# The order of the first attention pairs, and where V's parts and the weights' work are issued, in an attention-then-MLP kernel

## The chip, the core and the metric

The kernel runs on one core of a Trainium2 chip. The metric is the device time of one execution in microseconds (us); lower is better. The engines are named TensorE (PE), VectorE (DVE), ScalarE (ACT), GpSimd (POOL) and SyncE (SP); SP issues the DMAs.

## The reference

Windowed attention with a distance bias over 8 batches, 8 heads, 576 positions and head size 64, followed by an MLP on the 4608 tokens:

```python
scores = scale * q @ k.T                       # per batch and head
rel = pos[:, None] - pos[None, :]
scores = where((rel >= 0) & (rel < 128), scores - slope[h] * abs(rel), -1e9)
attn = softmax(scores)
x = (attn @ v).transpose(0, 2, 1, 3).reshape(4608, 512)
h = x @ w_in                                   # 512 -> 2048
g = h * sigmoid(h)
out = g @ w_out                                # 2048 -> 512
```

All inputs and the output are float32.

## The kernel before

The tokens are cut in 36 blocks of 128 (two batches make nine blocks). A *pair* p is four of the eight heads of block p // 2; there are 72 pairs. Four blocks (512 tokens) are a *group* g of the MLP; there are nine groups. The MLP of a group goes over 16 feature blocks f of 128: gemm1 makes h of the block in PSUM, act1 to act4 make g from it as a high part gh and a low part gl, and gemm2 adds the block's share to four PSUM banks w, x, y, z. Precision comes from splitting numbers in two parts and summing three products of parts.

Nothing is ordered by a scheduler. All is written out by hand as *steps*: `plan` maps a step's number to a list of functions, `put(step, fn, ...)` appends to it, `later(n, ...)` appends n steps ahead, and `begin()` issues the list of the present step. Each engine works its own instructions off in the order in which they were issued. Steps below 0 hold the attention of the first eight pairs alone (at(0) is step -82, each pair 8 steps on, at(7) is -26). From step 0 on, each step also holds half a gemm1 or half a gemm2, 64 steps to a group, while the attention of the next group's pairs runs between them. Within a step the functions of the pair loop come first, in order of the pairs, then those put further down.

A first pair (p < 8) goes through `scores` at n = at(p), `row_max` (adds the bias from `tab` and takes the maximum, VectorE), `exps` (ScalarE), `p_transpose_first` (TensorE, in float32, into PSUM bank h), `p_copy_first` (unit u = 0 on ScalarE, u = 1 on VectorE, into hl), `attend` (the products of the transposed weights with V and a column of ones, in float32) and `normalize`. The tiles t that row_max fills have three buffers, and a pair takes two. `x_transpose` then turns x for the first group, cc 0 and 1 from the even pairs' heads and 2 and 3 from the odd ones'; `x_low` makes its low part. Pairs from 8 on use halves in 16 bits instead: `p_hi`, `p_lo`, `p_transpose` (a DMA), and V in two parts, `v_hi` (GpSimd) and `v_lo` (VectorE). `load_v` brings V for them. Pair 8 starts at `CLOSE[0]`.

V's parts need a scale of V over a batch pair b: `vscale_load`, `vscale_reduce` (a chunk's maximum), and `vscale_finish` in three stages: reduce (VectorE, `vcol`), transpose (TensorE, `vt`, line 237) with a few small VectorE steps on one number, and a spreading matmul (TensorE, `vs`). `qk_load` and `qk_sum` gather statistics of q and k for later batches.

The 32 weight blocks are loaded and split while the first group's MLP runs, one by one, in the order of `wq`: `w_split1` and `w_low3` (ScalarE), `w_join` (VectorE), `w_hi` (ScalarE), `w_lo` (GpSimd). `w_next` starts one of them; `AHEAD` loads are issued before the MLP. At a group's last feature block, `turn_over` issues act2 to act4 and, where the next group needs it, `x_parts` at once.

The lines that set the order around the change:

```python
if p < 2 * GT:
    a = n + 2 * STEP + 1                         # attend of a first pair
put(n + STEP + 3, p_transpose_first, p, u)
put(n + STEP + 4, p_copy_first, p, u)
put(a - 3, v_hi, i); put(a - 2, v_lo, i)         # pairs from 8 on
seq += [("g1", n, 0)] + [("xt", 0, 2), ("xt", 0, 3)] * (n == 0) + [("g1", n, 1)]
if g == 0 and half == (n == 0):
    w_next()
```

Of the kernel before, what the change touches and what calls it, by code (L numbers as in the profile page):

```python
# [6 lines left out]
F32 = mybir.dt.float32  # L7
# [10 lines left out]
P = 128  # L18
# [36 lines left out]

IN16, OUT16 = 2, 3
QK16 = 2
STATS16 = ("w1_10", "w1_11")
RAW16 = ("w1_0", "w1_1")
Q16 = ("w1_2", "w1_3")  # L60
K16 = ("w1_4", "w1_5", "w1_6")
# [7 lines left out]
WHOLE = ("w1_12", "w0_13", "w0_14", "w1_13")  # L69
AHEAD = 12  # L70
KEPT = 6
WD = (1, 2, 3)

CLOSE = (1, 5, 8, 14, 20, 26, 32, 38)


def at(p):
# [9 lines left out]
def tile_window_attention_then_silu_mlp(ctx, tc, qk, qk16, v, w_in, w_out, base8, out):  # L87
# [86 lines left out]

    def vscale_load(b, i):

        t = early_tile(i) if b == 0 else pool.tile([P, DM], F32, tag="rv", bufs=2, name=f"vm{b}_{i}")
        nc.sync.dma_start(t, v[b, i * P : (i + 1) * P, :])
        vred.setdefault(b, {})[i] = t = t.rearrange("p (h d) -> p h d", h=H)
        if b == 0 and i < KEPT:  # L180
            rvs[i] = t

    def vscale_reduce(b, i):
# [6 lines left out]
        else:  # L190
            junk = pool.tile([P, H, D], F32, tag="gt", name=f"vj{b}_{i}")
            nc.scalar.activation(junk, t, AF.Abs, accum_out=m)

    def qk_load(b, i):

        if b == QK16:
            if i == 0:
                vred[b, "qk"] = pool.tile([P, 4, DM], F32, tag="xl", bufs=1, name=f"qs{b}")
            t = vred[b, "qk"][:, 2 * (i % 2) : 2 * (i % 2) + 2]
        else:  # L200
            t = pool.tile([P, 2, DM], F32, tag=STATS16[i % 2], bufs=1, name=f"qs{b}_{i}")
        nc.sync.dma_start(
            t.rearrange("p k (h c) -> p k h c", h=NHP), qk[b * NBLK + i].rearrange("k p h c -> p k h c")
        )
        vred[b, "qk", i] = t

    def qk_sum(b, i):

        t = vred.pop((b, "qk", i))
        for k in range(2):  # L210
            m = vred[b]["m"][:, (1 + k) * VCH + i : (1 + k) * VCH + i + 1]
            nc.scalar.activation(t[:, k], t[:, k], AF.Abs, accum_out=m)

    wsc = {}

# [9 lines left out]
    def vscale_finish(b, stage):  # L225

        if b >= QK16:
            scales16(b, stage)
            return
        r, name = vred[b], b  # L230
        if stage == 0:
            r["col"] = col = pool.tile([P, 3], F32, tag="vcol", name=f"vcol{name}")
            nc.vector.tensor_reduce(col[:, 0:1], r["m"], axis=AX.X, op=ALU.max)
        elif stage == 1:
            col = r["col"]
            ps = ps_of(next_tag("misc"), f"vt{name}")
            nc.tensor.transpose(ps[:1, :P], col[:, 0:1], ident)
            c = col[:1, 1:2]
            nc.vector.tensor_reduce(c, ps[:1, :P], axis=AX.X, op=ALU.max)
# [4 lines left out]
            nc.vector.tensor_scalar(c.bitcast(I32), c.bitcast(I32), -1, 268 << 23, op0=ALU.mult, op1=ALU.add)
        else:
            ps = ps_of(next_tag("misc"), f"vs{name}")
            nc.tensor.matmul(ps[:, 0:2], ones[:1, :], r["col"][:1, 1:3], start=True, stop=True)
            vsc[b] = pool.tile([P, 2], F32, tag="vsc", name=f"vsc{name}")
            nc.vector.tensor_copy(vsc[b], ps[:, 0:2])
            del vred[b]  # L250
# [255 lines left out]
    def attend(p):  # L506
        i, q = divmod(p, 2)
        o0 = blocks(p).start
        st[p]["av"] = av = ps_of(next_tag("av"), f"av{p}")[:, : 4 * (D + 1)].rearrange("p (h d) -> p h d", h=4)
        for u in range(2):  # L510
            if p < 2 * GT:
                for h in range(2):
                    for o in range(o0, 2):
                        nc.tensor.matmul(
                            av[:, 2 * u + h], st[p]["hl"][u][:, h * (2 - o0) + o - o0], vf[i - 1 + o][:, 4 * q + 2 * u + h],
                            start=o == o0, stop=o == 1, skip_group_check=True,
                        )
                continue
            hl = st[p]["hl"][u][:, : 4 * (2 - o0)].rearrange("p (a h o) r -> p a h o r", a=2, h=2)
            for h in range(2):  # L520
                seq = [
                    (hl[:, part, h, o - o0], vp[:, (i - 1 + o) % VSLOTS, 4 * q + 2 * u + h])
                    for o in range(o0, 2)
                    for part, vp in ((0, v1), (0, v2), (1, v1))
                ]
                for n, (lhs, rhs) in enumerate(seq):
                    nc.tensor.matmul(  # L527
                        av[:, 2 * u + h, : rhs.shape[-1]], lhs, rhs, start=(n == 0), stop=(n == len(seq) - 1),
                        skip_group_check=True,
                    )  # L530
# [276 lines left out]
    for p in range(NPAIR):  # L807
        i, q = divmod(p, 2)
        n = at(p)
        if p < 2 * GT:  # L810
            a = n + 2 * STEP + 1
        elif p == 2 * GT:
            a = n + 10
        elif p == 2 * GT + 1:
            a = n + 12
        else:
            a = n + (15 if p < 4 * GT else 13 if i < QK16 * NBLK else 12)
# [15 lines left out]
        if p < 2 * GT:  # L833

            for u in range(2):
                put(n + STEP + 3, p_transpose_first, p, u)
                put(n + STEP + 4, p_copy_first, p, u)
        else:
            put(n + 3, p_hi, p, 0)
            put(n + 4, p_lo, p, 0)  # L840
            put(n + 4, p_hi, p, 1)
            put(n + 4, p_transpose, p, 0)
            put(n + 5, p_lo, p, 1)
            put(n + 5, p_transpose, p, 1)
        put(a, attend, p)
        z = a + 1
        put(z, normalize, p, 0)
        put(z + 1, normalize, p, 1)
        put(z + 2, x_hi, p)
        put(z + 2, x_lo, p)  # L850
        if q == 0:
            if 1 < i < QK16 * NBLK:
                put(at(2 * i - 3) + 1, load_q, i)
                put(at(2 * i - 3) + 1, load_k, i)
            if i >= KEPT:
                put(n + 4, load_v, i)
            if i == GT:
                put(a - 5, v_hi, i - 1)
                put(a - 4, v_lo, i - 1)
            if i >= GT:  # L860
                put(a - 3, v_hi, i)
                put(a - 2, v_lo, i)
    for k in range(2 * NF):
        put(STATS + k, w_stat, k % 2, k // 2)
    for x, wait in enumerate((0, 2, 5)):
# [3 lines left out]
            for k, fn in enumerate((conv1, conv2, conv3)):  # L869
                put(n + SLICE * f + (CLEAR if f > 4 else 0) + (k if which or f else 0), fn, which, f)  # L870
    for g in range(1, NG):
        put(at(2 * GT * g) + 10, x_unit, g)
        if g >= IN16:
            put(g * SLICE * NF - 2, mlp_scales, g)
    for b in range(1, NBB):

        n = at(2 * GT * (NBLK * b // GT)) + 2
        for i in range(VCH):
            put(n - 53 + 5 * i, vscale_load, b, i)
            put(n - 49 + 5 * i, vscale_reduce, b, i)  # L880
            if b >= QK16:
                put(n - 52 + 5 * i, qk_load, b, i)
                put(n - 46 + 5 * i, qk_sum, b, i)
        for x, wait in enumerate((0, 2, 5)):
            put(n + wait, vscale_finish, b, x)

# [8 lines left out]
    def w_next_load():  # L895
        if wi[0] < len(wq):
            w_load(*wq[wi[0]])
            wi[0] += 1

    def w_next():  # L900
        if wi[1] < len(wq):
            a = wq[wi[1]]
            wi[1] += 1
            w_split1(*a)
            w_low3(*a)
            for fn, n in zip((w_join, w_hi, w_lo), WD):
                later(n, fn, *a)
            later(1, w_next_load)

    def begin():  # L910
# [3 lines left out]
    with tc.manual_schedule():  # L914
# [16 lines left out]
        for i in (2, 3):  # L931
            put(at(2 * i - 3) + 1, load_whole, i)
        for i in range(GT, VCH):
            put(at(4) + 3 + 3 * (i - GT), vscale_load, 0, i)
        for i in range(VCH):
            put(at(3) + 6 + 4 * i, vscale_reduce, 0, i)
        for x in range(3):
            put(at(7) + (6, 8, 16)[x], vscale_finish, 0, x)
        for n in range(AHEAD):
            put(at(1) + 4 + 5 * n, w_next_load)  # L940
        put(at(0) + 1, keep_warm, 6)
        put(at(1) + 1, keep_warm, 16)
        for n in (at(5) + 5, at(6) + 5, at(7) + 5):
            put(n, w_next)
        for cc in range(2):
            put(at(7) + 13 + cc, x_transpose, cc)
        put(at(7) + 14, x_low, 0)
        put(at(7) + 20, x_low, 1)
        while pos[0] < 0:
            begin()  # L950
            pos[0] += 1
# [2 lines left out]
        for g in range(NG):  # L954
# [2 lines left out]
            seq = []  # L957
            for f in range(NF):
                n = g * NF + f
                seq += [("g1", n, 0)] + [("xt", 0, 2), ("xt", 0, 3)] * (n == 0) + [("g1", n, 1)]  # L960
                if 0 < f < NF - 1:
                    seq += [("g2", n - 1, 0), ("g2", n - 1, 1)]
            n = g * NF + NF - 1
            seq += [("g2", n - 1, 0), ("g2", n - 1, 1), ("g2", n, 0), ("g2", n, 1)]
            for k, n, half in seq:
                if k == "xt":
                    x_transpose(half)
                    x_low(half)
                    continue
                begin()  # L970
                x_send()
                if k == "g1":
# [61 lines left out]
```

## Time and profile before

| what | value |
|---|---|
| median of 3 runs | 951.65 us (951.18 to 952.29) |
| the profiled execution | 949.61 us, span 947.8 us |
| TensorE busy | 921.9 us, 97% |
| VectorE busy | 655.0 us, 69% |
| ScalarE busy | 558.9 us, 59% |
| GpSimd busy | 133.5 us, 14% |
| DMA | 123.28 MB, mean 130 GB/s |
| chain that ended last | TensorE 78%, ScalarE 5%, VectorE 5%, issue 2% |

The span runs from the first to the last instruction of the program; the execution's time is a little longer. A row of a timeline gives start and duration in us, engine, line and operation, output <- input, the number of instructions merged in it, and in brackets how long the engine had been idle and what released it. Matmuls overlap in these rows, so their cost is read from start to start.

### The profile page before, as it was taken

The numbers are of one execution on the slowest core, as the hardware profiler recorded it, in microseconds if no ns is written. First come the engines' busy times: TensorE is split into PE (matmuls) and PEld (weight loads), VectorE is DVE, ScalarE is ACT, GpSimd is POOL, SyncE is SP. The second block draws the span as 40 slices with busy tenths as digits, with TensorE's granted clock in tenths as the row PEclk, the third lists the DMA queues.
The fourth block names the chain that finished last, engine by engine and source line by source line (L and its number), as shares of the span: only waits on it lengthen the run. The fifth ranks groups of instructions, "written<-read, shape, count | busy, mean of one in ns | idle before, by whom it ended". The sixth has DMA issues, their size and how long they took to land.

```text
span 947.8 us, 17110 instructions
## 1 busy us (share of the span) xinstructions
PE 921.9 (97%) x6442; PEld 574.9 (61%) x6442; DVE 655.0 (69%) x1603; ACT 558.9 (59%) x1152; POOL 133.5 (14%) x122
## 2 busy tenths in 40 slices
PE   8799999999999999999999999999999999999998
PEld 7677777777778888555545555555555545554443
DVE  4687887555778887899687778776777777743222
ACT  5678888676555674666567756555655565532222
POOL 0145665121212221000000000000000000000000
PEclk9999999999999999999999999999999999999999
DMA  9949942423277762644597765544654554421001
GB/s 277 375 119 246 272 101 67 106 65 87 65 181 200 166 142 50 156 101 101 111 244 179 221 144 132 118 112 98 139 111 104 119 142 106 87 55 56 1 1 44
DMA packets 209266, 123.28 MB, mean 130 GB/s; under 512 B 172576, under 2 KB 180768, under 8 KB 209184
## 3 DMA queue, kind: packets, MB, share of 16 engines
q1 hardware_dynamic: 209184, 122.19, 51.9%
q8 instruction: 50, 0.82, 0.4%
q14 instruction: 32, 0.26, 0.1%
HBM read 72.35 MB, written 9.44 MB: 86 GB/s over the span
## 4 chain that ended last, share of the span: by engine, by line
PE 78%; ACT 5%; DVE 5%; issue 2%; DMA 1%; POOL 1%; SPq 0%; DVEq 0%; ACTq 0%; POOLq 0%
PE o L700 34%; PE h L634 29%; PE h L639 6%; PE av L527 4%; PE sp L424 3%; PE sp L431 2%; DVE wm L742 1%; ACT t L463 1%; DVE t L453 1%; DVE gt L652 1%; ACT gt L647 1%; DVE x L137 1%; ACT wr L737 1%; ACT hr L472 1%; DVE v L406 1%
## 5 line engine op out<-in xcount | busy, mean ns | idle before, releaser
L700 PE MATMUL o<-w,gh 128*128 128x512 f16 (+1 forms) x1152 | 351.2, 386 | 1.4 <-ACT gh L660 1.4
L634 PE MATMUL h<-xt,w 128*128 128x512 f16 (+1 forms) x1536 | 310.6, 353 | 0.0
L647 ACT ACTIVATE gt<-h,gsc 128x512 f32<-128x512 f32 x112 | 77.0, 688 | 259.9 <-PE h L634 257.6
L700 PE MATMUL o<-w,gl 128*128 128x512 f16 (+1 forms) x576 | 221.8, 385 | 2.7 <-POOL gl L135 1.5
L634 PEld LDWEIGHTS <-w 128*128 128x128 f16 x1536 | 144.5, 98 | 125.8 <-issue 2.2
L652 DVE SCALAR_TENSOR_TENSOR gt<-gt,h 128x512 f32<-128x512 f32 x144 | 98.6, 685 | 122.6 <-ACT gt L647 122.1
L700 PEld LDWEIGHTS <-gh 128*128 128x128 f16 x768 | 74.8, 98 | 88.7
L463 ACT ACTIVATE t<-t,mx 128x256 f32<-128x256 f32 (+1 forms) x288 | 121.2, 487 | 12.3 <-DVE mx L453 12.1
L477 DVE SCALAR_TENSOR_TENSOR hr<-t,hr 128x512 f16<-128x512 f32 (+1 forms) x128 | 94.6, 741 | 23.5 <-ACT hr L472 23.3
L668 DVE SCALAR_TENSOR_TENSOR gl<-gt,gh 128x512 f16<-128x512 f32 x96 | 66.4, 692 | 53.9 <-ACT gh L662 51.3
L639 PE MATMUL h<-xh,w 128*128 128x512 f32 x256 | 90.0, 405 | 0.0
L400 POOL TENSOR_SCALAR v<-rv,vsc 128x512 f16<-128x512 f32 x30 | 24.4, 814 | 446.1 <-DMA rv<-v 233.1
L135 POOL TENSOR_TENSOR gl<-gt,gh 128x512 fp32r<-128x512 f32 x45 | 60.2, 1337 | 189.0 <-ACT gh L660 154.7
L700 PEld LDWEIGHTS o<-w,gh 128*128 128x128 f32 x384 | 69.9, 188 | 16.6 <-ACT gh L660 1.8
L472 ACT ACTIVATE hr<-t 128x512 f16<-128x512 f32 (+1 forms) x128 | 76.3, 601 | 1.0 <-DMA hl<-hr 1.0
L662 ACT ACTIVATE gh<-gt 128x512 f16<-128x512 f32 x96 | 60.2, 627 | 22.1 <-DVE gt L652 20.9
L700 PEld LDWEIGHTS <-gl 128*128 128x128 f16 x384 | 37.5, 98 | 47.9 <-DVE gl L668 3.5
L527 PEld LDWEIGHTS <-hl 128*128 128x128 f16 x1464 | 51.8, 98 | 22.4 <-issue 13.0
L453 DVE CUSTOM_DVE_ANT_0 t<-sp,tab,vsc 128x256 f32<-128x256 f32 (+1 forms) x144 | 58.6, 463 | 9.2 <-PE sp L424 8.8
L527 PE MATMUL av<-v,hl 128*128 128x65 f16 (+1 forms) x1464 | 55.8, 193 | 7.1 <-DVE v L406 5.7
L137 DVE SCALAR_TENSOR_TENSOR x<-xs,x 128x256 f16<-128x256 f32 x64 | 43.9, 687 | 24.0 <-ACT x L564 23.7
L453 DVE CUSTOM_DVE_ANT_0 t<-sp,tab 128x256 f32<-128x256 f32 (+1 forms) x144 | 50.5, 401 | 13.4 <-DMA tab<-base 7.1
(130 smaller groups left out, 1026.4 us busy)
## 6 DMA issues: line engine op xcount, KB each, us to landing
r<-qk SPq DMA_DIRECT2D x36, 512.0 KB, 4.2
out<-ot SPq DMA_DIRECT2D x36, 256.0 KB, 2.5
qs<-qk SPq DMA_DIRECT2D x18, 512.0 KB, 5.7
wr<-w_in SPq DMA_DIRECT2D x16, 512.0 KB, 7.3
wr<-w_out SPq DMA_DIRECT2D x16, 512.0 KB, 6.8
rv<-v SPq DMA_DIRECT2D x30, 256.0 KB, 3.1
vm<-v SPq DMA_DIRECT2D x27, 256.0 KB, 4.1
q<-qk SPq DMA_DIRECT2D x18, 256.0 KB, 3.6
```

Source lines behind the costliest of these rows:

```text
L135: engine.tensor_sub(out, a, b)
L453: nc.vector.tensor_tensor_reduce(out=t[:, h, 2 * P - n :], in0=st[p]["sp"][h][:, u, o].rearrange("p o c -> p (o c)"), in1=tab[:, 4 * q + 2 ...
L463: nc.scalar.activation(x, x, AF.Exp, bias=st[p]["mx"][:, 2 * u + h : 2 * u + h + 1], scale=-1.0)
L472: nc.scalar.activation(split_of(p, u, hr)[:, 0], t[:, :, 2 * P - n :], AF.Copy, scale=PSCALE)
L477: nc.vector.scalar_tensor_tensor(out=hr[:, 1], in0=t[:, :, 2 * P - n :], scalar=PSCALE, in1=hr[:, 0], op0=ALU.mult, op1=ALU.subtract)
L527: nc.tensor.matmul(av[:, 2 * u + h, : rhs.shape[-1]], lhs, rhs, start=(n == 0), stop=(n == len(seq) - 1), skip_group_check=True,)
L634: nc.tensor.matmul(o, w[:, wp, cc], x, start=start and k == 0, stop=stop, skip_group_check=True)
L639: nc.tensor.matmul(hps[n], w[:, cc], x, start=(half == 0 and i == 0), stop=(half == 1 and i == len(seq) - 1), skip_group_check=True,)
L647: nc.scalar.activation(gt, hps[n], AF.Tanh, scale=scale)
L652: nc.vector.scalar_tensor_tensor(out=gt, in0=gt, scalar=1.0, in1=hps[n], op0=ALU.add, op1=ALU.mult)
L668: nc.vector.scalar_tensor_tensor(out=gl, in0=gt, scalar=CUT, in1=gh, op0=ALU.mult, op1=ALU.subtract)
L700: nc.tensor.matmul(ops[ti], a[:, t], w, start=(f == 0 and i == 0), stop=(f == NF - 1 and i == len(seq) - 1), skip_group_check=True,)
```

## The change

- *First pairs.* The transposes of pair p-1 are issued right behind the scores of pair p, one unit after the other with its copy, and the products of pair p-2 behind them (`attend` two steps later; pairs 6 and 7 have steps of their own). Each product's moving operand is the same head of V twice, 130 columns instead of 65; the second result goes three places further in the PSUM bank, is overwritten there or never read.
- *x ahead of the MLP.* All four x_transposes and x_low come before step 0 instead of two of them between the halves of the first gemm1. Scores of pair 8 come at step -9 instead of 1.
- *V's scale of the first batch pair.* Its loads and reductions are spread over the first pairs, its stages come at -7, -6 and 3, with PSUM banks y and z; the weights' loads ahead start at at(2) + 2.
- *Weights.* Four of the weights' w_next come before the MLP, not three. Within a feature block, w_next runs in the first half of gemm1 and the second half of gemm2, and w_lo is entered in the plan by the new `w_rest`, behind what is already there.
- *V's parts.* From pair 8 on v_hi and v_lo are issued at a-5 and a-4 instead of a-3 and a-2 and load_v at n+1 instead of n+4.
- *Statistics.* V loads of batch pair 1 get a list of steps of their own (VM1); those of batch pair 3 use other buffers than the V blocks; qk_load is two DMAs of 256 KB with tiles of their own instead of one.

```diff
-CLOSE = (1, 5, 8, 14, 20, 26, 32, 38)
+CLOSE = (-9, 5, 8, 14, 20, 26, 32, 38)
+VM1 = (-1, 3, 7, 11, 15, 19, 24, 32, 37)
...
-            ps = ps_of(next_tag("misc"), f"vt{name}")
+            ps = ps_of("y" if b == 0 else next_tag("misc"), f"vt{name}")
...
     def attend(p):
-        st[p]["av"] = av = ps_of(next_tag("av"), f"av{p}")[:, : 4 * (D + 1)].rearrange("p (h d) -> p h d", h=4)
+        av = ps_of(next_tag("av"), f"av{p}")[:, : 7 * (D + 1)].rearrange("p (h d) -> p h d", h=7)
+        st[p]["av"] = av[:, :4]
...
-                            av[:, 2 * u + h], st[p]["hl"][u][:, h * (2 - o0) + o - o0], vf[i - 1 + o][:, 4 * q + 2 * u + h],
+                            av[:, 2 * u + h : 2 * u + h + 4 : 3], st[p]["hl"][u][:, h * (2 - o0) + o - o0],
+                            vf[i - 1 + o][:, head : head + 1].to_broadcast([P, 2, D + 1]),
...
-        if p < 2 * GT:
-            a = n + 2 * STEP + 1
+        if p == 2 * GT - 1:
+            a = n + 15
+        elif p < 2 * GT:
+            a = n + 2 * STEP + (2 if p == 2 * GT - 2 else 3)
         elif p == 2 * GT:
-            a = n + 10
+            a = n + 20
...
-                put(n + STEP + 3, p_transpose_first, p, u)
-                put(n + STEP + 4, p_copy_first, p, u)
+                m = n + STEP + (3 if p == 2 * GT - 1 else 1)
+                put(m, p_transpose_first, p, u)
+                put(m + u, p_copy_first, p, u)
...
-        put(z + 1, normalize, p, 1)
+        put(z + (p != 2 * GT - 1), normalize, p, 1)
...
-                put(n + 4, load_v, i)
+                put(n + 1, load_v, i)
             if i == GT:
-                put(a - 5, v_hi, i - 1)
-                put(a - 4, v_lo, i - 1)
+                put(a - 6, v_hi, i - 1)
+                put(a - 5, v_lo, i - 1)
             if i >= GT:
-                put(a - 3, v_hi, i)
-                put(a - 2, v_lo, i)
+                put(a - 5, v_hi, i)
+                put(a - 4, v_lo, i)
...
-            put(n - 53 + 5 * i, vscale_load, b, i)
-            put(n - 49 + 5 * i, vscale_reduce, b, i)
+            x = VM1[i] if b == 1 else n - 53 + 5 * i
+            put(x, vscale_load, b, i)
+            put(x + 4, vscale_reduce, b, i)
             if b >= QK16:
-                put(n - 52 + 5 * i, qk_load, b, i)
-                put(n - 46 + 5 * i, qk_sum, b, i)
+                put(n - 53 + 5 * i, qk_load, b, i)
+                put(n - 48 + 5 * i, qk_sum, b, i, 0)
+                put(n - 46 + 5 * i, qk_sum, b, i, 1)
...
+    def w_rest(f, which):
+        w_hi(f, which)
+        later(1, w_lo, f, which)
...
-            for fn, n in zip((w_join, w_hi, w_lo), WD):
-                later(n, fn, *a)
+            later(1, w_join, *a)
+            later(2, w_rest, *a)
...
-            put(at(4) + 3 + 3 * (i - GT), vscale_load, 0, i)
+            put(at(2) + 4 + 5 * (i - GT), vscale_load, 0, i)
         for i in range(VCH):
-            put(at(3) + 6 + 4 * i, vscale_reduce, 0, i)
+            put((-70, -64, -56, -48, -40, -34, -27, -14, -8)[i], vscale_reduce, 0, i)
         for x in range(3):
-            put(at(7) + (6, 8, 16)[x], vscale_finish, 0, x)
+            put((-7, -6, 3)[x], vscale_finish, 0, x)
         for n in range(AHEAD):
-            put(at(1) + 4 + 5 * n, w_next_load)
+            put(at(2) + 2 + 5 * n, w_next_load)
...
-        for n in (at(5) + 5, at(6) + 5, at(7) + 5):
+        for n in (at(4) + 5, at(5) + 5, at(6) + 5, -5):
             put(n, w_next)
-        for cc in range(2):
-            put(at(7) + 13 + cc, x_transpose, cc)
-        put(at(7) + 14, x_low, 0)
-        put(at(7) + 20, x_low, 1)
+        for cc, n in enumerate((-13, -12, -9, -9)):
+            put(n, x_transpose, cc)
+            put(n, x_low, cc)
...
-                seq += [("g1", n, 0)] + [("xt", 0, 2), ("xt", 0, 3)] * (n == 0) + [("g1", n, 1)]
+                seq += [("g1", n, 0), ("g1", n, 1)]
...
-                if g == 0 and half == (n == 0):
+                if pos[0] > 1 and g == 0 and half == (k == "g2"):
                     w_next()
```

More of the change, by code (lines that the diff above doesn't have):

```diff
@@ L57 @@
 QK16 = 2
-STATS16 = ("w1_10", "w1_11")
+STATS16 = (("w1_10", "w1_11"), ("w1_14", "w1_15"))
 RAW16 = ("w1_0", "w1_1")
@@ L71 @@
 KEPT = 6
-WD = (1, 2, 3)
-CLOSE = (1, 5, 8, 14, 20, 26, 32, 38)
+CLOSE = (-9, 5, 8, 14, 20, 26, 32, 38)
+VM1 = (-1, 3, 7, 11, 15, 19, 24, 32, 37)
 def at(p):
@@ L175, in vscale_load @@
     def vscale_load(b, i):
-        t = early_tile(i) if b == 0 else pool.tile([P, DM], F32, tag="rv", bufs=2, name=f"vm{b}_{i}")
+        if b == 0:
+            t = early_tile(i)
+        else:
+            tag, bufs = ("rv", 2) if b <= QK16 else (("w1_12", "w1_13")[i % 2], 1)
+            t = pool.tile([P, DM], F32, tag=tag, bufs=bufs, name=f"vm{b}_{i}")
         nc.sync.dma_start(t, v[b, i * P : (i + 1) * P, :])
@@ L192, in vscale_reduce, with stat_parts, qk_sum @@
             nc.scalar.activation(junk, t, AF.Abs, accum_out=m)
+    def stat_parts(b):
+        if (b, "parts") not in vred:
+            vred[b, "parts"] = pool.tile([P, 4, DM], F32, tag="xl", bufs=1, name=f"qs{b}")
+        return vred[b, "parts"]
     def qk_load(b, i):
[L196 to L209, printed above, removed]
-        for k in range(2):
-            m = vred[b]["m"][:, (1 + k) * VCH + i : (1 + k) * VCH + i + 1]
-            nc.scalar.activation(t[:, k], t[:, k], AF.Abs, accum_out=m)
+        for k in range(2):
+            if b == QK16:
+                t = stat_parts(b)[:, 2 * (i % 2) + k]
+            else:
+                t = pool.tile([P, DM], F32, tag=STATS16[k][i % 2], bufs=1, name=f"qs{b}_{i}_{k}")
+            nc.sync.dma_start(t.rearrange("p (h c) -> p h c", h=NHP), qk[b * NBLK + i, k])
+            vred[b, "qk", i, k] = t
+    def qk_sum(b, i, k):
+        t = vred.pop((b, "qk", i, k))
+        m = vred[b]["m"][:, (1 + k) * VCH + i : (1 + k) * VCH + i + 1]
+        nc.scalar.activation(t, t, AF.Abs, accum_out=m)
     wsc = {}
@@ L245, in vscale_finish @@
         else:
-            ps = ps_of(next_tag("misc"), f"vs{name}")
+            ps = ps_of("z" if b == 0 else next_tag("misc"), f"vs{name}")
             nc.tensor.matmul(ps[:, 0:2], ones[:1, :], r["col"][:1, 1:3], start=True, stop=True)
@@ L513, in attend @@
                     for o in range(o0, 2):
+                        head = 4 * q + 2 * u + h
                         nc.tensor.matmul(
-                            av[:, 2 * u + h], st[p]["hl"][u][:, h * (2 - o0) + o - o0], vf[i - 1 + o][:, 4 * q + 2 * u + h],
+                            av[:, 2 * u + h : 2 * u + h + 4 : 3], st[p]["hl"][u][:, h * (2 - o0) + o - o0],
+                            vf[i - 1 + o][:, head : head + 1].to_broadcast([P, 2, D + 1]),
                             start=o == o0, stop=o == 1, skip_group_check=True,
@@ L871, in tile_window_attention_then_silu_mlp @@
     for g in range(1, NG):
-        put(at(2 * GT * g) + 10, x_unit, g)
+        put(max(8, at(2 * GT * g) + 10), x_unit, g)
         if g >= IN16:
@@ L965, in tile_window_attention_then_silu_mlp @@
             for k, n, half in seq:
[L966 to L969, printed above, removed]
                 begin()
```

## The prediction

> **What bounds the kernel now.** I read the page's busy shares first, then TensorE's busy time by stretches, then the list of what TensorE waited for, and last the timelines of the engines at the places where those waits stand.
>
> ```profile
> span 947.8 us, 17110 instructions
> PE 921.9 (97%) x6442; PEld 574.9 (61%) x6442; DVE 655.0 (69%) x1603; ACT 558.9 (59%) x1152; POOL 133.5 (14%) x122
> ```
> ```profile
> 0.00:100.00 100.00, 87.47 (x663) 70.98 (x664) 68.72 (x211) 71.38 (x150) 33.35 (x36) 0.98 0.85 253
> ```
>
> TensorE (PE, the first busy number) is busy 921.9 of 947.8 us, so nothing but TensorE's own work and its 25.9 us of idle time can move the end. Nearly half of the idle time, 12.5 us, lies in the first 100 us, where the changed code runs. The waits name the rest:
>
> ```profile
> PE av L527 <- DVE v L406: 5.7, 6, 1.3
> PE vt L237 <- DVE vcol L233: 3.6, 1, 3.6
> ...
> PE sp L431 <- DVE xs L554: 1.7, 2, 0.9
> PE o L700 <- POOL gl L135: 1.5, 3, 0.6
> PE o L700 <- ACT gh L660: 1.4, 1, 1.4
> ```
> ```profile
> L514 PE MATMUL av<-vf,hl 128*128 128x65 f32 x112 | 14.8, 286 | 2.7 <-ACT hl L504 2.7
> ```
>
> The columns of a wait are total, times, longest. Four families matter: the low part of V (v_lo, 5.7 us, six times), the column of V's scale (3.6 us, once), the copies ahead of the first pairs' products (2.7 us, in the row of L514) and g's parts (gh, gl).
>
> **The first pairs' order.** This is one frame in the steady state, then the place where the frames end:
>
> ```profile
> 19.98 1.16 PE L431 MATMUL sp<-k,q 64*128 64x128 f32 x16
> 21.66 2.00 PE L514 MATMUL av<-vf,hl 128*128 128x65 f32 x16 [0.52 <-ACT hl L504]
> 23.49 1.04 PE L495 MATMUL pt<-ident,t 128*128 128x128 f32 x8
> 24.47 1.16 PE L431 MATMUL sp<-k,q 64*128 64x128 f32 x16
> ...
> 32.58 1.04 PE L495 MATMUL pt<-ident,t 128*128 128x128 f32 x8
> 37.26 0.27 PE L237 MATMUL vt<-ident,vcol 128*1 128x128 f32 x1 [3.64 <-DVE vcol L233]
> ```
>
> A frame lasts 4.49 us: scores 1.16, a wait of 0.52 for ScalarE's copy, products 1.83 from start to start, transposes 0.98. The products of pair p-2 wait for a copy that stands on ScalarE behind the exponentials of the frame before. After the change the order is scores of p, transposes of p-1, products of p-2, and the copies for those products were issued a whole frame earlier: the wait has nothing left to wait for. Also, the second row_max of pair p needs the t buffer that the transposes of p-1 free, and these now come ahead of the products, so the exponentials start sooner. All five waits go: -2.7 us. The frame is then 3.97 us of TensorE; per frame ScalarE has about 1.7 us of exponentials and a copy, and up to three weight passes and a reduction on top, which still fits with the slack of a frame.
>
> **Products of 130 columns.** 112 products issue 114 ns apart (1.83 us for 16) with 65 columns. The trace has no such product with 130 columns. From below: nothing, if the loading of 128x128 f32 weights sets the 114 ns. From above: scores have 128 columns of the same type on half the rows and run two row groups side by side; 16 of them take 1.16 us, so a pair of them at most 145 ns; that as the price of one product is 31 ns more, 112 of them 3.5 us. Less than nothing is excluded: columns are only added. Weights load for the next product while this one streams, as the 512-column matmuls show further on (two 0.62 us rows overlapping), so I take 5 ns each, 0.5 us. The Trainium skill, TensorE: Matmul & The Clock Gate, section LDWEIGHTS, gives a load as columns over 1.2 GHz, an estimate of 107 ns here, and its section on weight-path modes says that f32 gets no fast load; the 114 ns of the trace agree, and by that page the extra columns would be free and the sum 0.5 us better.
>
> **x whole ahead of the first matmul.** After the last transposes at 32.58 TensorE has 0.98 us of work and stands at 33.55; without the five waits at 30.85. Then come the products of pair 6 (1.83), transposes of pair 7 (0.98), two x_transposes (0.97, the row at 47.42 has four halves' worth of the same work), 0.3 for the copies that free bank h, products of pair 7 (1.83), scores of pair 8 (1.16) and two x_transposes (0.97): TensorE is through at 38.9. The old 3.64 us wait at 37.26 is gone from its place, since V's loads now stand between the weights' loads and the last V is five weights deep in the queue, not eight. But the vt transpose has been put at step -6, behind scores of pair 8, and on VectorE (DVE) the column it needs stands behind everything issued at -9 and -8:
>
> ```profile
> 47.42 1.03 PE L579 MATMUL xp<-ident,early 128*128 128x128 f32 x8
> 48.39 1.16 PE L431 MATMUL sp<-k,q 64*128 64x128 f32 x16
> ...
> 55.34 0.72 PE L700 MATMUL o<-w,gh 128*128 128x512 f32 x2 [1.41 <-ACT gh L660]
> 56.70 0.50 PE L700 MATMUL o<-w,gl 128*128 128x512 f32 x1 [0.63 <-POOL gl L135]
> ```
> ```profile
> 37.72 0.27 DVE L239 TENSOR_REDUCE vcol<-vt 1x1 f32<-1x128 f32 x1
> 38.55 0.14 DVE L244 TENSOR_SCALAR vcol<-vcol 1x1 int32<-1x1 int32 x1
> ...
> 48.68 1.29 DVE L584 TENSOR_TENSOR xl<-xp,xh 128x512 fp32r<-128x512 f32 x2 [1.88 <-ACT xh L580]
> 50.12 0.79 DVE L442 MEMSET sp<- 64x384 f32 x2 [0.15 <-issue]
> 50.81 0.41 DVE L453 CUSTOM_DVE_ANT_0 t<-sp,tab 128x256 f32<-128x256 f32 x1
> 52.19 0.67 DVE L652 SCALAR_TENSOR_TENSOR gt<-gt,h 128x512 f32<-128x512 f32 x1
> 57.66 0.79 DVE L477 SCALAR_TENSOR_TENSOR hr<-t,hr 128x512 f16<-128x512 f32 x1 [0.63 <-ACT hr L472]
> ```
> ```profile
> 48.06 1.07 ACT L580 CAST xh<-xp 128x512 fp32r<-128x512 f32 x2 [4.34 <-PE xp L579]
> ...
> 53.33 0.66 ACT L737 ACTIVATE wr<-wr 128x512 int32<-128x512 uint32 x1
> 53.88 0.90 ACT L463 ACTIVATE t<-t,mx 128x256 f32<-128x256 f32 x2
> 54.68 0.61 ACT L660 CAST gh<-gt 128x512 fp32r<-128x512 f32 x1
> 55.19 0.63 ACT L752 CAST w<-wm 128x512 fp32r<-128x512 f32 x1
> 55.71 0.60 ACT L647 ACTIVATE gt<-h 128x512 f32<-128x512 f32 x1
> ```
> ```profile
> 55.37 1.28 POOL L135 TENSOR_TENSOR gl<-gt,gh 128x512 fp32r<-128x512 f32 x1 [15.20 <-ACT gh L660]
> ```
>
> The third x_transpose ends near 38.6 with its latency, ScalarE's xh takes 0.6 more, then VectorE: two x_low 1.29, the two memsets of pair 8 0.79, four row_max 1.38 (50.81 to 52.19), the reduction 0.1: 42.8. So the wait is not removed but moved: I expect TensorE idle from 38.9 to 42.9 at L237, about 4 us. MLP's first matmul then starts at 43.0 instead of 45.14, and runs without the x_transposes (0.97), the scores (1.09) and the wait for xl that stood in it.
>
> Behind it the chain of ScalarE and VectorE decides, not TensorE. ScalarE: four exponentials until 43.65 (0.80 a pair, from 53.88 to 54.68), two p_hi 1.05, the weight's two passes 1.1: 45.8. VectorE: the scale's five small steps (about 1 us), two p_lo, then join 0.65: 46.45. ScalarE again: w_hi 0.52, tanh 0.52: 47.5. act2 0.65, meanwhile the next weight's two passes until 48.6, gh 0.5: 49.15, gl on GpSimd 1.28: 50.5. The first matmul with gl starts at 50.5 instead of 56.70: -6.2 us, with the 2.7 of the frames in it. With the products' 0.5 us: **-5.7 us**. Bounds: -2.5 with the products at their upper price and -7 with none and a VectorE that has half a microsecond less to do.
>
> The clock matters at this place:
>
> ```profile
> 38.00:39.00 1.00, 1.00 (x9) 1.00 (x9) 0.56 (x4) 0.62 (x1) 0.10 (x1) 0.76 1.09 378
> ...
> 42.00:43.00 1.00, 0.90 (x7) 0.52 (x5) 0.39 (x2) 0.59 (x1) 0.00 (x0) 1.00 1.03 394
> ```
>
> The number after the five engines is the granted clock. After the 3.64 us wait it fell, and it was back at 1.00 at 42. A wait of 4 us will do the same to the first 24 matmuls (5.6 us at full clock), some 1.5 us of delay; but gl is ready only at 50.5 and these would end at 50.2, so it costs nothing as long as that chain is as long as I make it. The Trainium skill, same page, section Why this matters for your kernels, warns of TensorE gaps over about 3 us for this reason; with a shorter chain its rule would take about 1.5 us from the gain.
>
> **V's parts two steps sooner.** Here the wait stands at a group's end:
>
> ```profile
> 470.50 0.69 DVE L652 SCALAR_TENSOR_TENSOR gt<-gt,h 128x512 f32<-128x512 f32 x1 [1.77 <-ACT gt L647]
> ```
> ```profile
> 166.67 0.77 PE L527 MATMUL av<-v,hl 128*128 128x64 f16 x20 [1.29 <-DVE v L406]
> 473.29 0.77 PE L527 MATMUL av<-v,hl 128*128 128x64 f16 x20 [0.90 <-DVE v L406]
> ```
>
> v_lo was issued behind turn_over (act2, act4 and x_parts of the group's last step) and so ran last. At a-4 it is issued ahead of turn_over, and VectorE sits idle there for 1.77 us, which holds its 0.75 us. load_v goes three steps up with it, ahead of the pair's DMA transposes on the SP queue, and v_hi comes two steps up on GpSimd, ahead of a group's last gl. Next late would be gl at the same turn, which in that timeline follows right behind act2 and is ready before TensorE gets there. All six waits go: **-5.7 us**. From the other side, if only the four of the later groups go (0.9 each): -3.6.
>
> **The weights' work behind gh, and the rest.** The second w_next of a feature block moves from one step ahead of gh to right behind it, w_lo behind gl on GpSimd. That is in the 50.5 above; the waits for gl later in the run are under 1 us and I leave them. The weights' loads start six steps later and the V's sooner; both stay ahead of use:
>
> ```profile
> qs<-qk SPq DMA_DIRECT2D x18, 512.0 KB, 5.7
> ...
> early<-v SPq DMA_DIRECT2D x5, 256.0 KB, 6.8
> ```
>
> The loads of the statistics become 36 of half the size: 18 more issues on SP, and nobody on the path waits for them. Should the V's land late (6.8 us from issue), the 4 us wait grows by as much. The V loads of batch 1 come earlier and cost nothing.
>
> **The sum.** -5.7 - 5.7 = -11.4 us on the profiled execution (949.61 us around a span of 947.8): 938.2. That execution lies 2.04 us below the median of the runs, 951.65, so for the median I say 940.3.
>
> **The rivals.** *The start doesn't move:* the wait at L237, with a slow clock behind it and landings of V later than I think, eats what the frames gain. For it speaks that the wait stays about as long; against it that 2.1 us of work leave the first feature block. Only V's waits go: 946.0. *V's waits come back elsewhere:* at the turn another wait (gl, a row_max) takes their place, only the start gains: 946.0. For it speaks that VectorE is 69% busy; against it the idle 1.77 us. *The products decide, and it gets slower:* if f32 streams 130 columns so that each product takes 100 ns more than now, 112 of them cost the whole 11.4 us; at 230 ns apiece, twice the time for twice the columns, 13 us, and the result is 953. Against it speak the scores' 145 ns. *Neither part bites:* 951.
>
> **How the numbers follow.** My forecast, a gain of 8 to 15 us, gets 0.68, the first rival 0.12, the second 0.11, the slower one 0.05, no change 0.04. A change within 0.2% (1.9 us) can't be told from none by such a measurement. The range goes from 935.5 (the better bound of the start, 1.3 us more, and the remaining waits for gl and xs with it) to 946.5 (one of the two gains missing). Faster 0.91, same 0.04, slower 0.05.
>
> **What would show it.** Right: no wait at L514 and L406, a wait of about 4 us at L237 near 39 us, the first L639 near 43 with twelve in a row, the first gl matmul near 50.5, products at most 120 ns apart. Wrong: products well over 120 ns apart; first L639 later than 45; the L527 waits there under another releaser.

## The result and the profile after

| | before | after |
|---|---|---|
| median | 951.47 us (951.18 to 952.29) | 958.47 us (957.39 to 961.38) |
| the profiled execution | 949.61 us, span 947.8 us | 961.38 us, span 959.6 us |

The change costs 7 us: the ratio of after to before is 1.0077, 95% interval 1.0054 to 1.0100. The forecast was 940.3 us, and none of the rivals named what happened. The profiled execution of after is the highest of its four, 2.9 us above their median, and that of before lies 2 us below its own, so differences of spans come out larger than 7.

The line numbers shift: L437 scores, L459 row_max, L501 first transposes, L522 first products, L536 later products, L563 normalize, L648 and L709 gemm1 and gemm2, L406 and L412 v_hi and v_lo, L739 to L751 w_split1, w_low3 and w_join, L761 w_hi, L669 gh, L677 act4 in 16 bits. L135 is a helper that GpSimd uses for gl and for w_lo alike; there the tile tells them apart.

The page of after, span and busy shares:

```profile
span 959.6 us, 17139 instructions
PE 927.1 (97%) x6442; PEld 576.8 (60%) x6442; DVE 654.2 (68%) x1603; ACT 557.9 (58%) x1152; POOL 134.7 (14%) x122
```

The shares look like those of before. The stretches do not. From 100 to 200 us, before and then after (five engines, granted clock, DMA share, GB/s):

```profile
100.00:200.00 100.00, 96.05 (x622) 74.86 (x621) 70.20 (x168) 77.68 (x170) 47.51 (x36) 1.00 0.50 124
```
```profile
100.00:200.00 100.00, 87.99 (x559) 67.03 (x560) 64.02 (x147) 71.07 (x149) 44.92 (x35) 0.98 0.42 113
```

TensorE loses 8 us of busy time there, and every other engine does less as well: no engine has become the bound, all of them wait. This is the MLP's first group, in which the weights are loaded and split. A mark for its end is the first `unit` step of V's scale on VectorE, before and then after:

```profile
165.29 0.16 DVE L334 TENSOR_TENSOR unit<-vsc,vsc 128x1 f32<-128x1 f32 x1
```
```profile
178.64 0.15 DVE L340 TENSOR_TENSOR unit<-vsc,vsc 128x1 f32<-128x1 f32 x1
```

The *start* is what lies ahead of the first matmul with gl; that matmul stands at 55.16 instead of 56.70. So the start gained 1.54 us, group 0 from there to the mark lost 14.9, and the 780 us behind it gave 1.5 back, which makes the 11.8 us between the spans. What TensorE of after waited for:

```profile
PE sp L437 <- DVE xs L563: 6.4, 6, 1.7
PE o L709 <- POOL w L135: 4.8, 4, 1.6
PE vt L243 <- DVE vcol L239: 3.9, 1, 3.9
PE av L536 <- DVE mx L459: 3.2, 3, 1.2
PE o L709 <- DVE gl L677: 2.7, 1, 2.7
PE o L709 <- ACT gh L669: 1.9, 1, 1.9
```

The six waits for v_lo of the products from pair 8 on are gone, as forecast. In their place stand waits for normalize (xs), row_max (mx), w_lo (w) and g's parts. All but the vt wait and the 2.7 lie in group 0.

### The profile page after: what moved, and what is told of

It is laid out like the page before. It is cut to its first block, busy times and chain, and to the rows that moved or that the text cites. A ratio compares the mean times of both kernels' runs of the same rounds, so it can differ in the third digit from the quotient of the medians.

```text
span 959.6 us, 17139 instructions
## 1 busy us (share of the span) xinstructions
PE 927.1 (97%) x6442; PEld 576.8 (60%) x6442; DVE 654.2 (68%) x1603; ACT 557.9 (58%) x1152; POOL 134.7 (14%) x122
## 4 chain that ended last, share of the span: by engine, by line
PE 77%; DVE 2%; issue 1%; ACT 1%; POOL 1%; DMA 1%; SPq 0%; POOLq 0%; ACTq 0%
PE o L709 35%; PE h L643 29%; PE h L648 5%; PE av L536 4%; PE sp L430 3%; PE sp L437 2%; DMA vm<-v 1%; POOL gl L135 0%; DVE gt L661 0%; DVE ot L719 0%; DVE hr L483 0%; ACT t L469 0%; DVE v L412 0%; ACT gh L669 0%; POOL w L135 0%
## 5 line engine op out<-in xcount | busy, mean ns | idle before, releaser
L709 PE MATMUL o<-w,gh 128*128 128x512 f16 (+1 forms) x1152 | 353.8, 388 | 6.7 <-POOL w L135 4.8
L709 PE MATMUL o<-w,gl 128*128 128x512 f16 (+1 forms) x576 | 222.6, 386 | 3.4 <-DVE gl L677 2.7
L709 PEld LDWEIGHTS <-gh 128*128 128x128 f16 x768 | 74.9, 98 | 89.0 <-issue 0.6
L677 DVE SCALAR_TENSOR_TENSOR gl<-gt,gh 128x512 f16<-128x512 f32 x96 | 67.1, 699 | 54.1 <-ACT gh L671 51.6
L648 PE MATMUL h<-xh,w 128*128 128x512 f32 x256 | 91.2, 410 | 0.0
L406 POOL TENSOR_SCALAR v<-rv,vsc 128x512 f16<-128x512 f32 x30 | 27.5, 916 | 431.2 <-DMA rv<-v 270.7
L135 POOL TENSOR_TENSOR gl<-gt,gh 128x512 fp32r<-128x512 f32 x45 | 58.4, 1297 | 193.4 <-ACT gh L669 142.3
L709 PEld LDWEIGHTS o<-w,gh 128*128 128x128 f32 x384 | 70.2, 189 | 24.1 <-POOL w L135 7.2
L709 PEld LDWEIGHTS <-gl 128*128 128x128 f16 x384 | 37.6, 98 | 50.2 <-DVE gl L677 5.5
L536 PEld LDWEIGHTS <-hl 128*128 128x128 f16 x1464 | 52.6, 99 | 18.5 <-issue 9.3
L459 DVE CUSTOM_DVE_ANT_0 t<-sp,tab,vsc 128x256 f32<-128x256 f32 (+1 forms) x144 | 58.5, 462 | 4.0 <-PE sp L430 3.7
L536 PE MATMUL av<-v,hl 128*128 128x65 f16 (+1 forms) x1464 | 55.9, 195 | 3.2 <-DVE mx L459 3.2
L648 PEld LDWEIGHTS h<-xh,w 128*128 128x128 f32 x256 | 48.8, 191 | 12.6 <-POOL w L135 0.4
```

Of the source, the lines that this page charges most:

```text
L459: nc.vector.tensor_tensor_reduce(out=t[:, h, 2 * P - n :], in0=st[p]["sp"][h][:, u, o].rearrange("p o c -> p (o c)"), in1=tab[:, 4 * q + 2 ...
L536: nc.tensor.matmul(av[:, 2 * u + h, : rhs.shape[-1]], lhs, rhs, start=(n == 0), stop=(n == len(seq) - 1), skip_group_check=True,)
L648: nc.tensor.matmul(hps[n], w[:, cc], x, start=(half == 0 and i == 0), stop=(half == 1 and i == len(seq) - 1), skip_group_check=True,)
L677: nc.vector.scalar_tensor_tensor(out=gl, in0=gt, scalar=CUT, in1=gh, op0=ALU.mult, op1=ALU.subtract)
L709: nc.tensor.matmul(ops[ti], a[:, t], w, start=(f == 0 and i == 0), stop=(f == NF - 1 and i == len(seq) - 1), skip_group_check=True,)
```

## Where group 0 loses its time

Two rows of the waits of all engines between 50 and 200 us lead there; before has neither:

```profile
ACT wm L739 <- POOL w L135: 18.6, 13, 2.0
DVE v L412 <- POOL v L406: 7.6, 6, 1.9
```

ScalarE stands 18.6 us before a weight's first pass because GpSimd's w_lo of an earlier weight isn't done. One turn of it, first GpSimd, then ScalarE, both of after (`issue` in brackets means that the profile names no releaser; gl's input gh comes from ScalarE):

```profile
85.03 1.31 POOL L135 TENSOR_TENSOR gl<-gt,gh 128x512 fp32r<-128x512 f32 x1 [3.26 <-issue]
86.29 1.72 POOL L135 TENSOR_TENSOR w<-wm,w 128x512 fp32r<-128x512 f32 x1
87.99 0.69 POOL L406 TENSOR_SCALAR v<-early,vsc 128x512 f16<-128x512 f32 x1
...
93.50 1.28 POOL L135 TENSOR_TENSOR gl<-gt,gh 128x512 fp32r<-128x512 f32 x1 [2.27 <-issue]
94.74 1.74 POOL L135 TENSOR_TENSOR w<-wm,w 128x512 fp32r<-128x512 f32 x1
```
```profile
91.81 0.62 ACT L761 CAST w<-wm 128x512 fp32r<-128x512 f32 x1 [1.25 <-DVE wm L751]
92.75 0.62 ACT L669 CAST gh<-gt 128x512 fp32r<-128x512 f32 x1 [0.31 <-DVE gt L661]
...
96.51 0.66 ACT L739 ACTIVATE wm<-wr 128x512 f32<-128x512 f32 x1 [1.21 <-POOL w L135]
```

w_hi ends at 92.43, and with it w_lo has its input. It starts at 94.74, because gl has been issued ahead of it and GpSimd works in order; gl waits for gh, which ends at 93.37, and starts at 93.50. w_lo then ends at 96.48, and 0.03 us later ScalarE's pass of another weight starts: it needs the wm buffer that w_lo reads (tag io, two buffers). Behind that pass stand the following tanh, exponentials and w_hi, which the next gh and the next w_lo need. The Trainium skill, PSUM — Partial Sum Buffer, section Engine vs sequencer instructions, says that the queues of ScalarE, VectorE and GpSimd are strictly first in, first out; the 2.3 us that this w_lo lost with its input ready agree.

The new `w_rest` makes this order: it enters w_lo in the next step's list from within a step, behind the gl that has been put there already. Before, w_lo was entered ahead of it.

## The experiments

Theory A: `w_rest`'s place for w_lo is the cause, by the chain above. Theory B: it is the pacing, a w_next behind gh in every other half, that crowds the engines. Theory C: V's parts, issued early, hold VectorE. Kernels whose label begins with b are built on before, the others on after.

**pace** and **rest**: the pacing alone put back, and w_lo alone put back.

```diff
pace:
-    if pos[0] > 1 and g == 0 and half == (k == "g2"):
+    if pos[0] > 1 and g == 0 and half == 0:
rest:
-    later(2, w_rest, *a)
+    later(2, w_hi, *a)
+    later(3, w_lo, *a)
```

> The changed kernel with the weights' w_next put back to the first half of every gemm1 and every gemm2 (two steps apart) in the first group; all else as changed. Theory 1 (pacing): w_next in two neighbouring steps asks for a third buffer of the two that w_split1 writes, so ScalarE waits for GpSimd's w_lo (18.6 us of such waits in the changed kernel), which holds up everything behind it in the first group. Then this wait is gone, the first group is 9 to 12 us shorter and the time is 946 to 950 us. Theory 2 (V's parts): v_lo now stands on VectorE while GpSimd has not finished v_hi (7.6 us of such waits) and holds up normalize and row_max; then this kernel stays at 956 to 959 us.

> The changed kernel with w_lo entered in the plan as before (three steps ahead by w_next itself, so in front of g's low part on GpSimd); the pacing stays as changed. Theory 1: ScalarE's wait for w_lo gets shorter by the 1.3 us of gl in each feature block but does not go: 951 to 956 us. Theory 2: no change, 957 to 960 us, perhaps with a new wait for gl.

pace took 962.11 us (1.0108, 1.0091 to 1.0125): B falls. rest took 940.73 us (0.9888, 0.9874 to 0.9903). Two lines turn +0.8% into -1.1%, and group 0's mark moves from 178.64 to 162.27 with the same start (first gl at 55.02). The two rows of waits in rest, 50 to 200 us:

```profile
DVE v L412 <- POOL v L406: 2.6, 6, 0.6
...
ACT wm L739 <- POOL w L135: 0.2, 1, 0.2
```

GpSimd's order in rest at the same feature block is w_lo, then gl, with no time lost between them:

```profile
88.83 1.30 POOL L135 TENSOR_TENSOR w<-wm,w 128x512 fp32r<-128x512 f32 x1 [1.28 <-ACT w L761]
90.07 1.29 POOL L135 TENSOR_TENSOR gl<-gt,gh 128x512 fp32r<-128x512 f32 x1
```

**b_rest**: before, with `w_rest` alone.

```diff
-    for fn, n in zip((w_join, w_hi, w_lo), WD):
-        later(n, fn, *a)
+    later(1, w_join, *a)
+    later(2, w_rest, *a)      # w_hi, then later(1, w_lo)
```

> The kernel before with the changed way to enter w_lo alone (w_hi enters it, behind gl); pacing and all else as before. Theory 1b: the same loop of waits between ScalarE and GpSimd, 960 to 970 us with more than 15 us of ScalarE waiting for w_lo. Rival (it hurts only with the paced w_next or with V's parts sooner): 951 to 954 us.

964.21 us (1.0131, 1.0101 to 1.0161): by itself this one edit makes the old kernel 12 us slower, and the mark is at 178.34. Its waits have the same signature, ScalarE's, and from TensorE's list the direct one:

```profile
ACT wm L730 <- POOL w L135: 22.8, 13, 2.2
```
```profile
PE o L700 <- POOL w L135: 8.1, 7, 2.4
```

**io3**: does the loss go through the two io buffers? They become three; the x tiles go from four to three buffers to make room, which had no run of its own. The first of the changed lines:

```diff
-m = pool.tile([P, DM], F32, tag="io", name=f"wm{f}_{which}")
+m = pool.tile([P, DM], F32, tag="io", bufs=3, name=f"wm{f}_{which}")
...
```

> The changed kernel as it is (w_lo behind gl), but with three buffers instead of two for what w_split1 writes (tag io), and three instead of four for the x tiles to make room. Theory 1b (ring): w_lo behind gl holds its buffer until gl is done, and gl waits for gh on ScalarE, so ScalarE's next w_split1 waits for GpSimd. With a third buffer ScalarE's waits for w_lo (18.6 us) fall under 5 us and the time is 940 to 946 us although w_lo stays behind gl. Rival (late weights): w_lo behind gl makes the weights' low parts late for gemm2 by themselves (4.8 us of such waits); then the third buffer changes little: 954 to 959 us.

952.44 us (0.9999, 0.9986 to 1.0011). ScalarE's row is gone, from 18.6 us to nothing, and the mark stands at 171.83. By the marks, of one profiled execution each, the ring of buffers carries 6.8 of the 16.4 us between after and rest. The late w_lo still hurts, since VectorE's wait is as long as in after:

```profile
DVE v L412 <- POOL v L406: 7.6, 6, 1.9
```

v_hi stands on GpSimd behind the late gl and w_lo, as the rows from 85.03 on show (gl, w_lo, v_hi); v_lo, issued early, waits for v_hi on VectorE and holds what is queued behind it: normalize and row_max, which TensorE's rows name.

**vold, io3_vold, b_v**: V's steps put back in after and in io3, and V's new steps alone in before.

```diff
vold, io3_vold (b_v the other way round), the lines for the pairs from 8 on:
-put(n + 1, load_v, i)
+put(n + 4, load_v, i)
-put(a - 5, v_hi, i); put(a - 4, v_lo, i)
+put(a - 3, v_hi, i); put(a - 2, v_lo, i)
...
```

> The changed kernel with V's parts and load_v at their old steps. Theory 1: the first group stays as slow and the waits of 0.9 us at the later groups' ends come back: 960 to 964 us. Theory 2: the first group is quick again: 949 to 953 us.

> Three buffers for w_split1, w_lo behind gl, V's parts at their old steps. Of the 18 us between the changed kernel and the one with w_lo as before, the third buffer gave 6. If the rest is v_lo on VectorE waiting for a v_hi that stands behind gl and w_lo on GpSimd (7 us of waits), then without V's move those waits go (under 2 us), the first group ends earlier, by 4 to 7 us, and V's waits at the later groups' ends (3.6 us and more) take part of it back: 948 to 952 us. If it is gemm2 waiting for late w_lo: 956 to 960 us.

> The kernel before with V's parts two steps sooner and load_v three steps sooner, nothing else. Theory 1: V's six waits go and nothing comes for them: 945 to 948 us. Theory 2: the first group gets slower, 953 to 957 us.

vold took 959.71 us (1.0087, 1.0072 to 1.0102): C doesn't explain the loss while ScalarE's loop stands, though the mark moves 3.9 us ahead, to 174.78. io3_vold took 950.61 (0.9967, 0.9954 to 0.9981); its mark is at 164.32, 7.5 us ahead of io3's, and its end gains less since the later groups' waits for v_lo are back (4.9 us, five times). So 6.8 us of group 0's 16.4 go through the buffers, 7.5 go once V's early steps are taken back too, and 2.1 are left between io3_vold and rest. The shares hold in this order only (without the third buffer V's old steps bring 3.9), and two smaller effects lie in them that no run separates: gemm2's own waits for w_lo (4.8 us in after, 3.6 in io3, 1.5 in io3_vold, none in rest), and v_lo itself, which takes longer in io3 (last section). That all of it begins with the late w_lo is shown by rest: V's steps are early there too, and the two rows of waits are down to 0.2 and 2.6 us. b_v took 950.99 (0.9996, 0.9986 to 1.0006). V's early steps are worth nothing in before: its waits for v_lo go, its mark moves from 165.29 to 171.59 (2.0 us of that by the first matmul with gl, at 58.71), and VectorE's row of waits is

```profile
DVE v L406 <- POOL v L400: 6.6, 5, 1.9
```

**rest_vold, rest_pace, rest_65, rest_qk, rest_start**: what the other parts are worth once w_lo is back in its place. The first takes V's steps back, the second the pacing, as above, each in rest. The other three edits:

```diff
rest_65:
-av[:, 2 * u + h : 2 * u + h + 4 : 3], ...
-vf[i - 1 + o][:, head : head + 1].to_broadcast([P, 2, D + 1]),
+av[:, 2 * u + h], ...
+vf[i - 1 + o][:, head],
rest_qk:
-put(n - 53 + 5 * i, qk_load, b, i)
+put(n - 52 + 5 * i, qk_load, b, i)
rest_start:
-put((-70, -64, -56, -48, -40, -34, -27, -14, -8)[i], vscale_reduce, 0, i)
+put((-70, -64, -56, -38, -40, -34, -27, -14, -18)[i], vscale_reduce, 0, i)
-put((-7, -6, 3)[x], vscale_finish, 0, x)
+put((-10, -9, 3)[x], vscale_finish, 0, x)
-for n in (at(4) + 5, at(5) + 5, at(6) + 5, -5):      # w_next
+for n in (at(4) + 5, at(5) + 5, at(6) + 5, -16):
```

> The changed kernel with w_lo entered as before and V's parts and load_v at their old steps. If V's steps are worth in this setting what the prediction gave them: 5 to 6 us more, 945.5 to 947 us. If the first group pays for it as it does in the kernel before (where the change of V's steps alone gave nothing): 940 to 942 us.

> The changed kernel with w_lo entered as before and w_next back at its even pace of two steps. Theory 1b says that the order of w_lo and gl is what hurts, and the kernel before with V's steps alone (gain 0.04%) says that V's steps need gh early: with w_next ahead of gh again, gl and so v_hi come later, v_lo waits for them on VectorE and the first group gives some 4 to 8 us back: 945 to 949 us. Rival (the pacing does nothing in itself): 940 to 942 us.

> The changed kernel with w_lo entered as before and products of 65 columns. If the 128x128 weight loads set the products' pace, as the 117 ns from start to start at 130 columns say: products at 114 to 117 ns, 940 to 941.5 us, no difference unless TensorE's clock falls in the first pairs (granted clock under 1.00 before 40 us), which would make it slower by 1 to 3 us.

> The changed kernel with w_lo as before and qk_load back one step, behind the V load of the same chunk by a step. If its bytes are what makes that V load land late (4.9 us against 3.3 us from issue) and so gl wait 1.6 us at 476 us: this wait falls to 0.8 us, 939.5 to 940.5 us. Rival: no change of the wait, the load is late because its issue stands behind DMA transposes.

> The changed kernel with w_lo as before and three moves ahead of the MLP: V's reduction of chunk 3 ten steps later (it holds VectorE for 2.7 us until a DMA lands), of chunk 8 ten steps sooner with the scale's first two stages at -10 and -9 (ahead of x_low and row_max of pair 8, so the 3.9 us wait at the vt transpose should go), the fourth w_next at -16. If these waits are what the start lost against the forecast: first matmul with gl 3 to 5 us earlier, 936 to 938.5 us. Rival (ScalarE's work ahead of the first tanh decides): gl moves by under 1.5 us, 939 to 941 us.

rest_vold took 947.68 us (0.9951, 0.9934 to 0.9968) with its six waits back, 5.5 us: V's steps are worth 0.6% here, some 6 us. rest_pace took 946.26 (0.9919, 0.9898 to 0.9940), its VectorE waiting 7.2 us for v_hi between 50 and 200 us: the intervals of it and of rest overlap a little, but against rest_qk, which ran in its session and is worth the same as rest, all four of its runs are slower, 3.7 us by the medians. The row shows what the pacing does. It keeps v_hi in time, and so lets V's early steps pay.

rest_65 took 941.19 (0.9894, 0.9860 to 0.9928), the same as rest. Products with 65 columns, then with 130 in after:

```profile
17.27 1.90 PE L522 MATMUL av<-vf,hl 128*128 128x65 f32 x16
19.10 1.16 PE L437 MATMUL sp<-k,q 64*128 64x128 f32 x16
```
```profile
17.43 1.95 PE L522 MATMUL av<-vf,hl 128*128 128x130 f32 x16
19.31 1.16 PE L437 MATMUL sp<-k,q 64*128 64x128 f32 x16
23.21 1.16 PE L437 MATMUL sp<-k,q 64*128 64x128 f32 x16
```

From start to start 114 and 117.5 ns a product: 0.05 us in a row of 16, 0.35 us for all 112. The granted clock is 1.00 from 10 to 40 us in both, so here the second half of the columns buys nothing.

rest_qk took 942.60 (0.9884, 0.9863 to 0.9905), the same as rest, and TensorE's wait for act4 (gl in 16 bits) at the turn near 478 us (a group's last feature block) stays at 1.63 us, though the statistics' loads now go out 3.1 us behind V's load instead of 0.6: they are not its cause. act4 stands on VectorE behind a reduction of V's maximum, which in both kernels sits 1.14 us until that load of V lands, 3.8 us after its issue. rest_start took 938.54 (0.9844, 0.9822 to 0.9867), the fastest kernel of the study; its lines stand in the next section.

## Why the prediction was wrong

**The step that failed.** It is the paragraph "The weights' work behind gh, and the rest": "w_lo behind gl on GpSimd. That is in the 50.5 above". It saw the move, and priced it at nothing but its share of the start. It didn't ask what has to be asked of a moved step: what stands ahead of w_lo in its new queue (a gl that waits for ScalarE), what w_lo holds (a buffer that ScalarE needs next, and v_hi behind it), and who stands behind those. rest against after puts it at 18 us, b_rest at 12 us in the old kernel. GpSimd's busy share gives no warning of this: 14% before and after (133.5 and 134.7 us).

**The waits for V.** "All six waits go: -5.7 us". They went, and in the right setting they were worth that: rest against rest_vold, some 6 us. The cover that the term named, 1.77 us of VectorE's idle time at a group's turn, was right for the later groups. In group 0 the price depends on v_hi being early, which the prediction put down as "ahead of a group's last gl" without asking after GpSimd's queue within a feature block; b_v and rest_pace show the 6.6 and 7.2 us of VectorE's waits that come there. "Next late would be gl at the same turn [...] ready before TensorE gets there" missed by little: in rest TensorE waits 1.63 us for act4 at that turn, where before's longest such wait was 0.8.

**The start.** The forecast of -5.7 us measured -1.5. The frames were right where nothing disturbs them: scores stand 3.90 us apart (19.31 and 23.21 above; the forecast 3.97), and the products at 117.5 ns against a taken 119. (The sum's own terms give bounds of -2.7 and -6.7, not -2.5 and -7; the measured gain lies outside both pairs.) Then waits that the sum left out follow, in after on VectorE, ScalarE and TensorE:

```profile
21.64 0.69 DVE L193 TENSOR_REDUCE vmx<-vf 128x1 f32<-128x512 f32 x1 [2.71 <-DMA vf<-v]
```
```profile
23.70 0.62 ACT L761 CAST w<-wm 128x512 fp32r<-128x512 f32 x1 [3.19 <-DVE wm L751]
```
```profile
25.26 0.83 PE L501 MATMUL pt<-ident,t 128*128 128x128 f32 x4 [0.89 <-ACT t L469]
...
41.88 1.09 PE L588 MATMUL xp<-ident,early 128*128 128x128 f32 x8
46.89 0.27 PE L243 MATMUL vt<-ident,vcol 128*1 128x128 f32 x1 [3.91 <-DVE vcol L239]
46.91 0.50 PE L648 MATMUL h<-xh,w 128*128 128x512 f32 x1
...
55.16 0.50 PE L709 MATMUL o<-w,gl 128*128 128x512 f32 x1
```

A reduction of V's maximum, moved to a step at which its chunk hasn't landed, held VectorE for 2.71 us, w_join behind it, ScalarE's w_hi behind that, and the exponentials behind w_hi; TensorE felt it as a wait for t. That chunk's load keeps its step (issued at 14.59 us; 15.26 in before) and lands 7.0 us later. The prediction looked at the moved loads ("both stay ahead of use") and asked after a late landing of V only at the end of the chain, at the vt wait, not at the reductions that come sooner. The last x_transposes end at 42.97 instead of the forecast 38.9. The wait at L237 (now L243) is as forecast, 3.91 us for about 4, but 4 us later, so the first gemm1 comes at 46.91: the prediction's own sign of being wrong, later than 45. The stretch behind it took 8.27 us against 7.6. The slow clock there, of which the prediction said that "it costs nothing as long as that chain is as long as I make it", has a part in that: TensorE has no gap from 46.89 to 55.16, at a granted clock of 0.72 from 45 to 50, and ScalarE's first tanh (51.54) waits 0.47 us for gemm1. rest_start tests these waits: it issues that reduction ten steps later and takes the scale's column and one weight off the place where they are waited for.

```profile
41.05 0.27 PE L243 MATMUL vt<-ident,vcol 128*1 128x128 f32 x1
...
41.95 0.47 PE L648 MATMUL h<-xh,w 128*128 128x512 f32 x1
...
49.90 0.74 PE L709 MATMUL o<-w,gh 128*128 128x512 f32 x2 [1.60 <-ACT gh L669]
51.25 0.80 PE L709 MATMUL o<-w,gl 128*128 128x512 f32 x1 [0.61 <-POOL gl L135]
...
56.46 0.39 PE L648 MATMUL h<-xh,w 128*128 128x512 f32 x1
```

The same two places in rest:

```profile
55.02 0.50 PE L709 MATMUL o<-w,gl 128*128 128x512 f32 x1
...
58.72 0.40 PE L648 MATMUL h<-xh,w 128*128 128x512 f32 x1
```

The vt wait is gone, and gl's first matmul starts at 51.25, 3.8 us ahead of rest's 55.02. A third of that is lost at once: the same matmuls up to the next gemm1 take 5.21 us instead of 3.70, without another gap, at a granted clock of 0.66 between 50 and 55 (rest: 1.00 from 55 to 60). At the mark 2.6 us are left (159.68 against 162.27), and 2.6 at the end by the spans (936.6 against 939.2); by the medians of one session rest_start is 4.1 us ahead of rest_qk.

**What rest's 940.7 doesn't prove.** It falls on the forecast 940.3, partly by luck. By the spans, on which the sum was made, rest is 8.6 us ahead of before, not 11.4: the start gave 1.7 of its 5.7, group 0 gave 1.3, the rest of the run 5.6. By the medians of its session it is 11.0 us ahead, since the profiled execution of before lay 2 us below its median. It is rest_start, 11.2 us by the spans (14.6 by the medians of its session), that reaches the forecast sum, and it isn't the change as made.

**The rivals.** The first, a start that doesn't move, is what happened to the start; its 946.0 missed the rest. The second, V's waits coming back elsewhere, is what b_v shows, though it named TensorE's waits at the turn and not GpSimd's queue; here it is a part of a larger loop. The slower rival named the products, which the 117.5 ns exclude. The slower rival that was missing was the queue of GpSimd.

## What to carry to other kernels

When an instruction is moved on an engine that works in order, read what now stands ahead of it and what that waits for, and which buffer it frees and for whom: an engine with 14% of busy time can hold three others through a ring of two buffers. Where an edit consists of several moves, look for the one that changes the order of two instructions on the same queue, not only their step, and price it by the wait of the one that is now ahead. A consumer that is issued earlier needs all its producers earlier too, not only the load: v_lo with a late v_hi held everything behind it on VectorE.

## What the hardware showed beside

In this kernel a product with f32 weights of 128x128 costs 114 ns with 65 columns and 117.5 with 130, where bounds from the scores had allowed 31 ns more.

A v_lo that starts just behind a w_lo (or a gl) on GpSimd takes 1.77 us instead of 0.75. In io3, VectorE and GpSimd:

```profile
87.43 1.77 DVE L412 SCALAR_TENSOR_TENSOR v<-early,vsc,v 128x512 f16<-128x512 f32 x1 [1.51 <-POOL v L406]
```
```profile
87.36 1.29 POOL L135 TENSOR_TENSOR w<-wm,w 128x512 fp32r<-128x512 f32 x1
```

The Trainium skill, SBUF — State Buffer, section SBUF: two separate sides, says that a VectorE operation with two inputs in SBUF and a GpSimd operation share a port, and that the one that starts first keeps it for its whole instruction. These rows agree: w_lo ends at 88.65 and v_lo 0.55 later, at 89.20. Of the six v_lo of group 0, four are that long in io3, five in b_v and in rest_pace, three in before, one in after and none in rest. So GpSimd's order can cost VectorE 1.0 us a time, beside the waits for v_hi.

The clock fell after shorter waits than the one that the prediction weighed. After TensorE's wait of 1.90 us for gh at 176.47 it was, in after:

```profile
176.00:178.00 2.00, 1.53 (x4) 1.01 (x5) 1.55 (x4) 2.00 (x4) 0.00 (x0) 0.74 0.00 0
178.00:180.00 2.00, 2.00 (x20) 1.39 (x20) 1.24 (x7) 2.00 (x6) 0.00 (x0) 0.50 0.00 0
180.00:182.00 2.00, 2.00 (x19) 1.74 (x17) 1.59 (x3) 1.96 (x4) 0.00 (x0) 0.91 0.05 12
```

In rest_start the two waits of 1.60 and 0.61 us, both between 48.3 and 51.25, left a clock of 0.66 from 50 to 55. Before's waits of 1.41 and 0.63 us at the same place left it at 1.00 up to 60, and so did rest's single wait of 1.63 us at 478. What sets the limit, these runs don't show.
